# Two attentions, twice over: more of the second attention's exponentials on VectorE, by masks, under new order rules

## The chip, the cores and the metric

The kernel runs on one core of a Trainium2 chip. The metric is the device time of one execution in microseconds (us). A core has engines that run side by side, each with its own queue worked in order: TensorE (PE in the profile; PEld is its weight load), VectorE (DVE), ScalarE (ACT), GpSimd (POOL), and SyncE (SP), which here issues the DMA transfers. TensorE writes its results to PSUM, eight banks of 128 x 512 fp32; VectorE and ScalarE read them there and write to SBUF.

## The reference

x is 2048 rows of 1024 features. Four blocks follow each other; each adds its result to x. Blocks 1 and 3 are a linear attention with learned feature maps ("A"), blocks 2 and 4 a softmax attention ("B"); both use 32 heads of 32 features, and the same weights in both rounds.

```python
def _A_ref(x, wqkv, w_phi, wo):
    ...
    pq = jnp.einsum("bhsd,hdf->bhsf", q, w_phi)
    pk = jnp.einsum("bhsd,hdf->bhsf", k, w_phi)
    phi_q = jnp.concatenate([_softmax(pq, axis=-1), _softmax(-pq, axis=-1)], axis=-1)
    phi_k = jnp.concatenate([_softmax(pk, axis=-1), _softmax(-pk, axis=-1)], axis=-1)
    kv = jnp.einsum("bhsf,bhsd->bhfd", phi_k, v)
    ...
def _B_ref(x, wqkv, wo):
    ...
    scores = jnp.einsum("bhqd,bhkd->bhqk", q, k) * (Dh ** -0.5)
    p = _softmax(scores, axis=-1)
    o = jnp.einsum("bhqk,bhkd->bhqd", p, v)
    return (lambda x, *d: x.transpose(*d))(o, 0, 2, 1, 3).reshape(B, S, D) @ wo
x = x + _A_ref(_layernorm(x, axis=-1), A_wqkv, A_w_phi, A_wo)
x = x + _B_ref(_layernorm(x, axis=-1), B_wqkv, B_wo)
x = x + _A_ref(_layernorm(x, axis=-1), A_wqkv, A_w_phi, A_wo)
x = x + _B_ref(_layernorm(x, axis=-1), B_wqkv, B_wo)
```

## The kernel before

**A planner sets the order.** The body records operations (`op`: engine, planned duration, dependencies, buffers, a priority `prio`) and `Sched.run` (L145) plays them against a model of the engines: whenever an engine is free it takes the ready operation of the lowest `prio` whose buffers can be had, unless its priority lies more than WINDOW beyond the earliest work not yet begun. The order in which operations were picked is the order in which the instructions are then written, so every engine's queue is fixed beforehand. The planned durations (`act_us`, `dve_us`, `MM`) serve this order alone. Priorities count in planned microseconds of the stage: a softmax attention starts at `at`, and each of its turns is 10 units. QUOTA limits how many buffers of a class live at once. Operations marked `first` (the score groups, from the third on) go ahead of all others on TensorE. Where the plan has TensorE less than KEEP busy over SPELL, it puts in matmuls that add zero to an open accumulator (`idle_acc`, L1290).

**Two rounds of two stages.** A round ("layer") is a linear attention and then a softmax attention. The reference's 2048 rows are worked in four chunks of 512 (`qc` for queries). The keys and key states of the next round's linear attention for three chunks (`layernorm` and `a_keys` with `alone`) run inside the first softmax attention, as do its output projections.

**The softmax attention.** The 32 heads are eight groups `g` of four. A turn is one chunk of queries and one group: (qc, g). Before, the turns go over all groups with chunks 0 and 1, then chunk 2 over all groups, then chunk 3 (`turns`, L1137). A turn has two half-turns `pp`, each with eight steps d of four score tiles j: 64 tiles of 128 keys x 512 queries. A score tile is one matmul with 32 rows (row-tiled; four of them fit the array side by side). Tiles are taken in threes: three matmuls (L1034) into three banks (0 to 2 or 3 to 5 in turn), then one exponential on ScalarE of 128 x 1536 (L1042). The accumulation (L1072) multiplies the exponentials with the values and with ones, four column-tiled matmuls a step, into bank 6; at the end of a half-turn VectorE copies it to SBUF (L1087), the sums of the exponentials go through DRAM (rd) to be inverted and spread, and L1128 divides.

**Everything else passes bank 7.** Projections for later groups (`b_k`, `b_v`, `b_q`), output projections (`b_o`, in the last round `b_last`) and the next round's keys are column-tiled matmuls (L438) into bank 7 (`FIL`), read by VectorE (L867 and others). `q_away` (L884) computes the queries of chunks 2 and 3 early and stores them in DRAM (qd), `q_back` fetches them. Weights come as slabs (`slab`; class "w2" for 128 columns of a projection).

**VectorE's exponentials.** `EXTRA` names, for each turn of each round, pairs (pp, d): the two tiles j = 3 of steps d and d + 1 are taken off ScalarE's list and made by `exp_dve` (L959): a single score matmul into bank 7 (L972) for each, two operations of VectorE that read the bank (L977, L980), then six over both tiles (L983, L986, three times L991, L994). They round the scaled score to a multiple, evaluate a polynomial of the rest, and multiply by a power of two made with integer arithmetic.

Of the kernel before, what the change touches and what calls it, by code (L numbers as in the profile page):

```python
# [11 lines left out]
ALU = mybir.AluOpType  # L12
# [22 lines left out]
class Op:  # L35
    __slots__ = ("eng", "dur", "lat", "fn", "bufs", "prio", "mode", "ndep", "out", "t", "start", "seq", "accum", "first")

    def __init__(self, eng, dur, lat, fn, bufs, prio, mode, seq):
        self.eng, self.dur, self.lat, self.fn, self.bufs = eng, dur, lat, fn, bufs
        self.prio, self.mode, self.seq = prio, mode, seq  # L40
        self.ndep, self.out, self.t, self.start, self.accum, self.first = 0, [], 0.0, None, None, False
# [6 lines left out]
class Sched:  # L48
# [11 lines left out]
    def op(self, eng, dur, fn, deps=(), bufs=(), prio=0.0, lat=None, mode=None):  # L60
# [5 lines left out]
        for b in o.bufs:  # L66
            b.left += 1
        self.ops.append(o)
# [76 lines left out]
    def run(self):  # L145
# [21 lines left out]
        for o in self.ops:  # L167
            if o.ndep == 0:
                heapq.heappush(ready[o.eng], (not o.first, o.prio, o.seq, o))
        t, left, order = 0.0, len(self.ops), []  # L170
        while left:
            moved = False
            for e in engines:
# [29 lines left out]
                if pick is None:  # L203
                    continue
                if e == "PE":
# [28 lines left out]
            while events and events[0][0] <= t + 1e-9:  # L234
# [6 lines left out]
                for x in o.out:  # L241
# [4 lines left out]
                    if x.ndep == 0:  # L246
                        heapq.heappush(ready[x.eng], (not x.first, x.prio, x.seq, x))
# [10 lines left out]
LNN = 4  # L258
GATE = (1, 1)
KVG = 0.12  # L260
QUOTA = {"pk": 3, "pv": 2, "kv": 1, "ln": 2, "mm": 2, "cmp": 2, "bc": 4, "num": NUMS, "wt": 4, "fil": 2,
         "e": 6, "vp": 6, "e1": 4, "vp1": 4, "E": 6, "q2": 3, "kt": 3, "w2": 8, "w2o": 3, "oT": 26, "T": 4, "den": 2,
         "lnt": 6, "lnw": 2, "lnw1": 1, "eq": 8, "ns": 4, "cw": 6, "hl": 6, "oc": 2, "slab": 7, "slabk": 3, "fin": 4,
         "rs": 8, "pkf": 1, "cden": 2, "part": 8, "w2r": 1,
         "xs": 1, "xu": 2, "xg": 2, "xx": 2, "E1": 3}
# [3 lines left out]
ROUND = 1.5 * 2**21  # L269
POW2_D = 0.32318750170670074  # L270
POW2_0 = 0.998010015430466
POW2_C = (-2.753493604392706, 3.611980637904819, -2.738565741928622)
# [17 lines left out]
def kernel(  # L290
# [20 lines left out]
    q_scale = float(DH**-0.5 / (4 * math.log(2)))  # L311
# [379 lines left out]
    def mmg2(pb, pv, lhs, rhs, d1, d2, bufs, prio, lo=0, hi=4, more=False):  # L691
# [267 lines left out]
    def exp_dve(qc, g, pp, d, prio, kT, q_of):  # L959


        u_b, u_v = sb("xu", 2, C512, dt=F32)
        g_b, g_v = sb("xg", 2, C512, dt=F32)
        x_b, x_v = sb("xx", 2, C512, dt=F32)
        e_b, e_v = sb("E1", 2, C512)
        r = slice(96, 128)
        gs = []
        for k in range(2):
            s_b, s_v = ps("xs", FIL)

            def sfn(k=k, s_v=s_v):
                nc.tensor.matmul(  # L972
                    out=s_v(), lhsT=kT[g][1]()[r, pp, (d + k) * P:(d + k + 1) * P],
                    rhs=q_of[(qc, g)][1]()[r, (pp + 1) % 2, :], start=True, stop=True, tile_position=(96, 0))
            so = op("PE", MM, sfn, flat([kT[g][2][(d + k) // 2], q_of[(qc, g)][2]]),
                    [s_b, kT[g][0], q_of[(qc, g)][0]], prio, mode="r")
            uo = op("DVE", dve_us(512), lambda k=k, s_v=s_v: nc.vector.tensor_scalar(  # L977
                out=u_v()[:, k, :], in0=s_v(), scalar1=POW2_D, scalar2=ROUND, op0=ALU.add, op1=ALU.add),
                [so], [s_b, u_b], prio + 0.01)
            gs.append(op("DVE", dve_us(512), lambda k=k, s_v=s_v: nc.vector.scalar_tensor_tensor(  # L980
                out=g_v()[:, k, :], in0=u_v()[:, k, :], scalar=ROUND, in1=s_v(), op0=ALU.subtract, op1=ALU.subtract),
                [uo], [s_b, u_b, g_b], prio + 0.01))
        wo = op("DVE", 1024 / 1920 + 0.15, lambda: nc.vector.tensor_scalar(  # L983
            out=u_v(), in0=u_v(), scalar1=ROUND - 31.5, scalar2=ROUND + 32.0, op0=ALU.max, op1=ALU.min),
            gs, [u_b], prio + 0.02)
# [340 lines left out]
```

## Time and profile before

| | us |
|---|---|
| median of 3 runs (lowest to highest) | 2449.53 (2446.66 to 2449.86) |
| profiled execution, its own time | 2446.52 |
| its span, first to last instruction | 2444.7 |
| busy in it: TensorE / VectorE / ScalarE | 2298.8 / 1337.6 / 2128.3 |
| L1042, ScalarE's exponentials, 1332 of them | 1798.7 |
| first and last start of L1042 in the first softmax attention | 354.3 and 1308.5 |
| first and last start of L1042 overall | 354.3 and 2430.7 |

A row of a group reads: line, engine, operation, output and input tile, shapes, how often; then busy time in us and mean of one in ns; then the idle time of the engine just before them and what ended it. A row of a stretch gives its bounds and length, then the busy time of each engine with the number of instructions in brackets, the granted TensorE clock, the DMA share and GB/s. TensorE's busy time includes matmuls that overlap each other and the added zeros, so it isn't a measure of need.

### The profile page before, as it was taken

The numbers are of one execution on the slowest core, as the hardware profiler recorded it, in microseconds if no ns is written. First come the engines' busy times: TensorE is split into PE (matmuls) and PEld (weight loads), VectorE is DVE, ScalarE is ACT, GpSimd is POOL, SyncE is SP. The second block draws the span as 40 slices with busy tenths as digits, with TensorE's granted clock in tenths as the row PEclk, the third lists the DMA queues.
The fourth block names the chain that finished last, engine by engine and source line by source line (L and its number), as shares of the span: only waits on it lengthen the run. The fifth ranks groups of instructions, "written<-read, shape, count | busy, mean of one in ns | idle before, by whom it ended". The sixth has DMA issues, their size and how long they took to land.

```text
span 2444.7 us, 65791 instructions
## 1 busy us (share of the span) xinstructions
PE 2298.8 (94%) x29160; PEld 848.7 (35%) x29160; DVE 1337.6 (55%) x1775; ACT 2128.3 (87%) x1891; POOL 22.0 (1%) x70
## 2 busy tenths in 40 slices
PE   7999999999989999899999999999999998998998
PEld 4443333333333333333333333333333333333333
DVE  6986752222256635533425766322255478788863
ACT  6336569999999999999996555799999999999998
POOL 0000000000000000000000000000000000000000
PEclk9999999999999999999999999999999999999999
DMA  9210101112111122222324001111121100100000
GB/s 208 62 36 3 31 20 39 39 42 51 37 58 45 45 65 76 75 71 72 123 59 125 1 5 40 32 43 37 40 64 28 37 30 26 35 31 28 27 23 32
DMA packets 204773, 118.59 MB, mean 49 GB/s; under 512 B 122824, under 2 KB 194504, under 8 KB 203720
## 3 DMA queue, kind: packets, MB, share of 16 engines
q1 hardware_dynamic: 203432, 112.29, 17.0%
q8 instruction: 228, 3.74, 0.6%
q10 hardware_dynamic: 1056, 2.10, 0.3%
q14 instruction: 57, 0.47, 0.1%
HBM read 78.71 MB, written 16.24 MB: 39 GB/s over the span
## 4 chain that ended last, share of the span: by engine, by line
ACT 43%; PE 35%; issue 10%; DVE 7%; DMA 3%; SPq 2%; ACTq 0%; DVEq 0%
ACT arena L1042 42%; PE psum L434 19%; PE psum L1072 5%; PE psum L438 4%; PE psum L1034 4%; DVE arena L991 2%; DMA arena<-rd 1%; SPq L469 1%; PE psum L1290 1%; DVE arena L1128 1%; ACT arena L638 1%; PE psum L804 1%; PE psum L671 1%; DVE arena L977 1%; DVE arena L1087 1%
## 5 line engine op out<-in xcount | busy, mean ns | idle before, releaser
L1042 ACT ACTIVATE arena<-psum 128x1536 bf16<-128x1536 f32 x1332 | 1798.7, 1677 | 15.1 <-PE psum L1034 7.6
L1072 PE MATMUL psum<-arena 128*32 128x512 bf16 x4096 | 657.1, 385 | 8.8 <-DVE arena L1087 4.9
L1072 PE MATMUL psum<-arena,ones_bf 128*32 128x512 bf16 x4096 | 656.8, 386 | 2.3 <-issue 2.3
L1034 PE MATMUL psum<-arena 32*128 32x512 bf16 x3996 | 525.1, 383 | 97.1 <-ACT arena L1042 88.9
L438 PE MATMUL psum<-arena 128*32 128x512 bf16 x8256 | 578.6, 381 | 3.8 <-DVE arena L530 0.8
L434 PE MATMUL psum<-arena 128*128 128x512 bf16 x2032 | 472.5, 384 | 10.5 <-DVE arena L1108 3.1
L1034 PEld LDWEIGHTS <-arena 32*128 32x128 bf16 x3996 | 175.5, 91 | 624.6 <-issue 613.1
L434 PEld LDWEIGHTS <-arena 128*128 128x128 bf16 x2032 | 191.0, 98 | 268.7 <-issue 58.2
L438 PEld LDWEIGHTS <-arena 128*32 128x32 bf16 x8256 | 204.1, 96 | 211.4 <-issue 64.8
L1072 PEld LDWEIGHTS <-arena 128*32 128x32 bf16 x4096 | 156.4, 94 | 277.7 <-issue 250.8
L867 DVE CAST arena<-psum 128x512 bf16<-128x512 f32 x112 | 77.2, 689 | 259.2 <-PE psum L438 246.2
L991 DVE SCALAR_TENSOR_TENSOR arena<-arena 128x1024 f32<-128x1024 f32 x150 | 183.4, 1222 | 7.4 <-PE psum L438 2.5
L1290 PE MATMUL psum<-xT,zero 128*32 128x512 bf16 x2296 | 182.9, 380 | 0.0
L1072 PEld LDWEIGHTS <-ones_bf 128*32 128x32 bf16 x4096 | 153.9, 94 | 16.1 <-issue 7.4
L1087 DVE COPY arena<-psum 128x512 f32<-128x512 f32 x126 | 86.6, 687 | 97.3 <-PE psum L1072 96.2
L1128 DVE TENSOR_TENSOR arena<-arena 64x512 bf16<-64x512 f32 x124 | 84.6, 682 | 59.5 <-DMA arena<-rd 46.7
L638 ACT ACTIVATE arena<-psum 128x512 bf16<-128x512 f32 x80 | 42.8, 598 | 79.4 <-PE psum L434 65.7
L651 DVE TENSOR_TENSOR arena<-psum,arena 128x1024 bf16<-128x1024 f32 x64 | 78.3, 1224 | 59.2 <-PE psum L438 53.2
L977 DVE TENSOR_SCALAR arena<-psum 128x512 f32<-128x512 f32 x100 | 68.9, 689 | 69.9 <-PE psum L972 61.8
L642 DVE TENSOR_REDUCE arena<-arena 128x32 f32<-128x1024 bf16 x64 | 77.7, 1214 | 48.6 <-ACT arena L638 48.6
L761 ACT ACTIVATE arena<-psum 128x512 bf16<-128x512 f32 x128 | 69.4, 595 | 34.1 <-PE psum L434 33.6
L526 DVE TENSOR_TENSOR arena<-xT,arena 128x1024 f32<-128x1024 bf16 x64 | 77.9, 1218 | 31.3 <-ACT arena L515 31.2
(102 smaller groups left out, 1295.9 us busy)
## 6 DMA issues: line engine op xcount, KB each, us to landing
arena<-rd SPq DMA_DIRECT2D x62, 256.0 KB
arena<-in_A_wqkv_dram SPq DMA_DIRECT2D x10, 1024.0 KB
arena<-in_B_wqkv_dram SPq DMA_DIRECT2D x32, 256.0 KB
arena<-arena SPq DMA_DIRECT2D x256, 32.0 KB
arena<-in_B_wo_dram SPq DMA_DIRECT2D x32, 256.0 KB
arena<-wd_k SPq DMA_DIRECT2D x8, 1024.0 KB
arena<-in_B_wqkv_dram SPq DMA_DIRECT2D x4, 1024.0 KB
arena<-arena SPq DMA_DIRECT2D x64, 64.0 KB
```

The costliest lines, as they stand in the source:

```text
L434: nc.tensor.matmul(out_, lhsT=lhsT, rhs=rhs, start=start, stop=stop, skip_group_check=True)
L438: nc.tensor.matmul(out_[ks, :], lhsT=lhsT[:, ks], rhs=rhs, start=start, stop=stop, tile_position=(0, 32 * k), skip_group_check=True)
L526: s1 = op("DVE", dve_us(1024), lambda pr=pr, w_v=w_v: nc.vector.tensor_tensor(out=w_v(), in0=xT[:, pr, csl(c)], in1=m_v().unsqueeze(1).to_ ...
L651: ml = op("DVE", dve_us(1024), lambda vpv=vpv, wv_=wv_, sv=sv: nc.vector.tensor_tensor(out=wv_()[:, :, :, 0:DH], in0=vpv().rearrange("p (h ...
L977: uo = op("DVE", dve_us(512), lambda k=k, s_v=s_v: nc.vector.tensor_scalar(out=u_v()[:, k, :], in0=s_v(), scalar1=POW2_D, scalar2=ROUND, o ...
L991: last = [op("DVE", dve_us(1024), lambda i=i, c=c: nc.vector.scalar_tensor_tensor(out=x_v(), in0=(x_v() if i else g_v()), scalar=c, in1=g_ ...
L1034: nc.tensor.matmul(out=s_v()[:, x * C512:(x + 1) * C512], lhsT=kT[g][1]()[r, pp, d * P:(d + 1) * P], rhs=q_of[(qc, g)][1]()[r, (pp + j // ...
L1042: ex = op("ACT", act_us(w * C512), lambda s_v=s_v, e_v=e_v, w=w: nc.scalar.activation(out=e_v()[:, 0:w * C512], in_=s_v(), func=ACT.Exp, s ...
L1072: nc.tensor.matmul(out=a_v()[col:col + 32, :], lhsT=v_v()[:, kc % 4, o:o + DH] if what == 0 else ones_bf[:], rhs=ev()[:, x * C512:(x + 1) ...
L1087: cp = op("DVE", dve_us(512), lambda t_v=t_v, a_v=a_v: nc.vector.tensor_copy(out=t_v(), in_=a_v()), [last], [a_b, t_b], prio - 4)
L1128: s = [op("DVE", dve_us(512), lambda a=a, k=k, o_v=o_v, r_v=r_v, T=T: nc.vector.tensor_tensor(out=o_v()[a, :], in0=T[k][1]()[a, :], in1=r_ ...
L1290: nc.tensor.matmul(psum[32 * k:32 * k + 32, 6 * C512:7 * C512], lhsT=zero[:], rhs=xT[:, 0, 0:C512], start=False, stop=False, tile_position ...
```

## The change

- `exp_dve`: the score plus a constant is written straight as an integer whose bits are the fp32 number with the right exponent and a linear mantissa (one operation per tile reads the bank, in place of two). One operation masks the mantissa and sets the exponent of 1, one masks the exponent; a polynomial of three steps and a last multiplication follow. The scale of scores changes with it (`q_scale`, and `scale` of ScalarE's exponential).
- The pair is the two tiles j = 2, 3 of one step d, in place of j = 3 of two steps. Their accumulation steps go to the end of their half-turn.
- `EXTRA`: first softmax attention 10 pairs before, 37 after; second 40 before, 54 after.
- Order rules: VectorE's operations that read banks 6 and 7 count as 20 units earlier (`EVAC`); the later steps of a begun projection into bank 7 count as 20 earlier (`BOOST`); the single scores (`along`) may only be taken while TensorE is in row-tiled mode, or when overdue, and then rank with the score groups.
- Turns: `SIDE` chunks go side by side over the groups, 2 in the first softmax attention (as before), 3 in the second. In the second the queries of the last chunk are computed late and are no longer put away in DRAM; weights for it, and for those put away in the first, are loaded once more.
- Times of projections (`QA`, `VGAP`, `LATE`, `BO`, `OP0`, `OGAP`), quotas and the planned duration `KVG` differ.

```diff
@@ Sched.op
+        if eng == "DVE" and any(b.kind == "ps" and b.banks in ([(7,)], [(6,)]) for b in o.bufs):
+            o.ahead = EVAC
@@ Sched.run
-                heapq.heappush(ready[o.eng], (not o.first, o.prio, o.seq, o))
+                heapq.heappush(ready[o.eng], (not (o.first or o.along), o.prio - o.ahead, o.seq, o))
...
-                    if item[1] <= todo[front] + WINDOW and self._alloc(item[3].bufs):
+                    if item[3].along and mode[e] != item[3].mode and item[3].prio > now - DUE:
+                        skipped.append(item)
+                        continue
+                    if item[3].prio <= todo[front] + WINDOW and self._alloc(item[3].bufs):
...
+                if pick.first:
+                    now = pick.prio
@@
-KVG = 0.12
+DUE = 0.0
+BOOST = 20.0
+EVAC = 20.0
+QA = (40.0, 7.0)
+KVG = 0.14
...
-         ... "w2": 8, ... "oT": 26, ... "xu": 2, "xg": 2, "xx": 2, "E1": 3}
+         ... "w2": 6, ... "oT": 27, ... "xu": 2, "xg": 1, "xx": 1, "E1": 3}
...
-EXTRA = (lambda i: [(0, 2), (1, 2)] if 12 <= i < 17 else [],
-         lambda i: ([(0, 2), (1, 2)] if i % 3 else [(0, 2), (0, 5), (1, 4)]) if 16 <= i < 30 else [(i % 2, 2)] if 8 <= i < 16 else [])
+SIDE = (2, 3)
+VGAP = 7.0
+LATE = 10.0
+BO = 225
+OP0 = (233, 259, 285)
+OGAP = (3.2, 3.2, 3.2)
+EXTRA = (lambda i: [(0, 2), (1, 2)] if 10 <= i < 19 else [(1, 2)] if 2 < i < 31 else [],
+         lambda i: [(0,2),(1,4)] if 3 <= i < 30 else [])
@@ mmg2
+            if cols and i > lo:
+                last.ahead = BOOST
@@ exp_dve
-        r = slice(96, 128)
+                r = slice(64 + 32 * k, 96 + 32 * k)
...
-            so = op("PE", MM, sfn, flat([kT[g][2][(d + k) // 2], q_of[(qc, g)][2]]),
+            so = op("PE", 0.05, sfn, flat([kT[g][2][d // 2], q_of[(qc, g)][2]]),
                     [s_b, kT[g][0], q_of[(qc, g)][0]], prio, mode="r")
-            uo = op("DVE", dve_us(512), ... scalar1=POW2_D, scalar2=ROUND, op0=ALU.add, op1=ALU.add),
-            gs.append(op("DVE", dve_us(512), ... scalar=ROUND, in1=s_v(), op0=ALU.subtract, op1=ALU.subtract),
-        wo = op("DVE", 1024 / 1920 + 0.15, ... op0=ALU.max, op1=ALU.min),
-        wo = op("DVE", 1024 / 1920 + 0.15, ... op0=ALU.subtract, op1=ALU.mult), [wo], [u_b], prio + 0.02)
+            so.along = True
+            ys.append(op("DVE", dve_us(512), lambda k=k, s_v=s_v: nc.vector.tensor_scalar(
+                out=y_v()[:, k, :].bitcast(I32), in0=s_v(), scalar1=POW2_B, scalar2=0.0, op0=ALU.add, op1=ALU.max),
+                [so], [s_b, y_b], prio + 0.01))
+        mo = op("DVE", 1024 / 1920 + 0.15, lambda: nc.vector.tensor_scalar(
+            out=m_v().bitcast(I32), in0=y_v().bitcast(I32), scalar1=0x7FFFFF, scalar2=0x3F800000,
+            op0=ALU.bitwise_and, op1=ALU.bitwise_or), ys, [y_b, m_b], prio + 0.02)
+        po = op("DVE", 1024 / 1920 + 0.15, lambda: nc.vector.tensor_scalar(
+            out=y_v().bitcast(I32), in0=y_v().bitcast(I32), scalar1=0x7F800000, scalar2=None,
+            op0=ALU.bitwise_and), [mo], [y_b], prio + 0.02)
@@ attention
-                    for d in range(8):
+                    own = extra(pos[(qc, g)])
+                    order = [(d, u) for d in range(8) for u in range(2) if not (u and (pp, d) in own)]
+                    order += [(d, 1) for d in range(8) if (pp, d) in own]
+                    for n, (d, u) in enumerate(order):
@@ the rounds
+        turns = [(qc, g) for g in range(G) for qc in range(wide)] + [(qc, g) for qc in range(wide, NC) for g in range(G)]
...
-                    away = q_away(g, qc, pr + 2 + 6 * (qc - 2), w, FIL)
+                elif wide == 2:
+                    pl = at + QA[0] + QA[1] * (2 * g + qc - 2)
+                    if qc == 2:
+                        wl = slab("w2", pl - 4, B_w[:, :, g * P:(g + 1) * P], P, [away])
+                    away = q_away(g, qc, pl, wl, FIL)
                     q_of[(qc, g)] = q_back(g, qc, at + 10 * pos[(qc, g)] - 12, away)
+        if wide == 3:
+            for g in range(G):
+                pl = at + 10 * pos[(NC - 1, g)] - LATE
+                after = q_of[(NC - 1, g - 2) if g > 1 else (2, G - 1)][2][0]
+                wl = slab("w2", pl - 3, B_w[:, :, g * P:(g + 1) * P], P, [after])
+                q_of[(NC - 1, g)] = b_q(g, NC - 1, pl, wl, FIL)
...
-            bo_s = [slab("slab", at + 160 + fc, ...
+            bo_s = [slab("slab", at + BO + fc, ...
...
-                gap = (6, 6, 9)[qc]
-                p0 = (163, 200, 251)[qc]
+                gap = OGAP[qc]
+                p0 = OP0[qc]
```

More of the change, by code (lines that the diff above doesn't have):

```diff
@@ L35 @@
 class Op:
-    __slots__ = ("eng", "dur", "lat", "fn", "bufs", "prio", "mode", "ndep", "out", "t", "start", "seq", "accum", "first")
+    __slots__ = ("eng", "dur", "lat", "fn", "bufs", "prio", "mode", "ndep", "out", "t", "start", "seq", "accum", "first", "ahead", "along")
     def __init__(self, eng, dur, lat, fn, bufs, prio, mode, seq):
@@ L246, in run @@
                     if x.ndep == 0:
-                        heapq.heappush(ready[x.eng], (not x.first, x.prio, x.seq, x))
+                        heapq.heappush(ready[x.eng], (not (x.first or x.along), x.prio - x.ahead, x.seq, x))
         self.end = t
@@ L309 @@
     assert D == 1024 and S % C512 == 0
[L311 removed]
+    q_scale = float(DH**-0.5 / math.log(2) * BITS)
     A_w = A_wqkv.rearrange("(po pi) f -> pi po f", pi=P)
@@ L983, in exp_dve @@
-        wo = op("DVE", 1024 / 1920 + 0.15, lambda: nc.vector.tensor_scalar(
-            out=u_v(), in0=u_v(), scalar1=ROUND - 31.5, scalar2=ROUND + 32.0, op0=ALU.max, op1=ALU.min),
-            gs, [u_b], prio + 0.02)
-        wo = op("DVE", 1024 / 1920 + 0.15, lambda: nc.vector.tensor_scalar(
-            out=u_v().bitcast(I32), in0=u_v(), scalar1=ROUND - 31.75, scalar2=float(2**25),
-            op0=ALU.subtract, op1=ALU.mult), [wo], [u_b], prio + 0.02)
-        last = gs
+            so.along = True
@@ L1042, in attention @@
             ex = op("ACT", act_us(w * C512), lambda s_v=s_v, e_v=e_v, w=w: nc.scalar.activation(
-                out=e_v()[:, 0:w * C512], in_=s_v(), func=ACT.Exp, scale=4 * math.log(2)),
+                out=e_v()[:, 0:w * C512], in_=s_v(), func=ACT.Exp, scale=math.log(2) / BITS),
                 [so], [s_b, e_b], prio - 3)
@@ L1133, in attention @@
         return oTs, so
-    turns = [(qc, g) for g in range(G) for qc in range(2)] + [(qc, g) for qc in range(2, NC) for g in range(G)]
-    pos = {t: i for i, t in enumerate(turns)}
     xnA, xnB = {}, {}
@@ L1161 @@
         base = BASE[layer]
+        wide = SIDE[layer]
+        turns = [(qc, g) for g in range(G) for qc in range(wide)] + [(qc, g) for qc in range(wide, NC) for g in range(G)]
+        pos = {t: i for i, t in enumerate(turns)}
         second = base + (100, 45)[layer]
```

74 lines of the change are left out of this document (35 added, 39 removed).

## The prediction

> **What bounds the kernel now.** I read the page's busy strips first, then stretches of the span, then the groups by line and shape, then one piece of timeline.
>
> ```profile
> DVE  6986752222256635533425766322255478788863
> ACT  6336569999999999999996555799999999999998
> ```
>
> Two plateaus of nines on ACT are the two softmax attentions; the low parts before them are the linear attentions. The plateaus, asked as stretches (length; then busy time of PE, PEld, DVE, ACT):
>
> ```profile
> 354.30:1310.70 956.40, 896.30 (x13050) 316.28 (x13047) 389.74 (x518) 941.66 (x737) 8.31 (x24) 1.00 0.23 64
> 1540.30:2432.30 892.00, 836.71 (x11549) 290.40 (x11551) 526.46 (x676) 886.04 (x664) 0.00 (x0) 1.00 0.12 34
> ```
>
> ScalarE idles only 14.7 us and 6.0 us in them, so they last as long as ScalarE's list of work. That list is L1042, exponentials of three score tiles at once:
>
> ```profile
> L1042 ACT ACTIVATE arena<-psum 128x1536 bf16<-128x1536 f32 x1332 | 1798.7, 1677 | 15.1 <-PE psum L1034 7.6 <-PE psum L1072 7.4
> L977 DVE TENSOR_SCALAR arena<-psum 128x512 f32<-128x512 f32 x100 | 68.9, 689 | 69.9 <-PE psum L972 61.8 <-ACT arena L1042 5.8 <-PE psum L1072 1.1
> L980 DVE SCALAR_TENSOR_TENSOR arena<-arena,psum 128x512 f32<-128x512 f32 x100 | 68.7, 687 | 4.2 <-PE psum L1072 0.2
> L986 DVE TENSOR_SCALAR arena<-arena 128x1024 int32<-128x1024 f32 x50 | 34.6, 693 | 1.5
> L991 DVE SCALAR_TENSOR_TENSOR arena<-arena 128x1024 f32<-128x1024 f32 x150 | 183.4, 1222 | 7.4 <-PE psum L438 2.5 <-PE psum L1072 1.3 <-PE psum L1034 0.3
> L972 PE MATMUL psum<-arena 32*128 32x512 bf16 x100 | 38.5, 385 | 3.4 <-DVE arena L867 2.8 <-DVE arena L980 0.4
> L1087 DVE COPY arena<-psum 128x512 f32<-128x512 f32 x126 | 86.6, 687 | 97.3 <-PE psum L1072 96.2 <-ACT arena L1042 0.3
> ```
>
> One exponential is listed with 1.677 us, but neighbours overlap: the stretch 1940 to 2210 us is 270.00 us of ScalarE without a gap and touches 203 of them, some 202.5 whole, so a triple adds 1.333 us. The VectorE lines are its own exponentials and the reading of accumulators (L1087). VectorE is far from full on average; where the kernel before is densest in its exponentials, the stretch reads
>
> ```profile
> 2000.00:2360.00 360.00, 327.27 (x4468) 112.42 (x4461) 305.26 (x378) 359.35 (x269) 0.00 (x0) 1.00 0.09 29
> ```
>
> VectorE 85% busy, ScalarE without a gap worth the name. TensorE is close behind ScalarE, as one period of timeline shows:
>
> ```profile
> 2100.34 0.39 PE L1034 MATMUL psum<-arena 32*128 32x512 bf16 x3
> ...
> 2101.10 0.60 PE L438 MATMUL psum<-arena 128*32 128x512 bf16 x8
> ...
> 2101.64 0.39 PE L1034 MATMUL psum<-arena 32*128 32x512 bf16 x3
> ```
>
> From scores to scores 1.30 us, in which two accumulation steps and two projection steps ran, 0.217 us each (a step is four column-tiled matmuls). So scores and their mode switch take 1.30 - 4 x 0.217 = 0.43 us, and a triple of ScalarE covers (1.333 - 0.43)/0.217 = 4.2 steps.
>
> **ScalarE's list.** The table of pairs gives VectorE 37 pairs in place of 10 in the first attention, 54 in place of 40 in the second. A pair is two of 2048 score tiles. First: (74 - 20)/3 = 18 triples fewer, x 1.333 = -24.0 us. Second: (108 - 80)/3 = 9.33, x 1.333 = -12.4 us. The built program agrees: 1332 triples become 1304 and one double. Together -36.4 us, all on the path.
>
> **VectorE's pair.** Before: 2 x 0.689 + 2 x 0.687 + 2 x 0.693 + 4 x 1.222 = 9.03 us. After: two reads of a bank (as L977, 0.689), a mask-and-set and a mask over 1024 int32, four scalar_tensor_tensor (1.222). No row shows a bitwise operation; the nearest are L986 (one source, int32 out, 0.693) and L991 (1.222). I take 0.693, since it too has one source: 7.65 us; with the other it is 8.71. VectorE then has 390 - 90 + 283 = 583 us in about 930 (63%) and 526 - 361 + 413 = 578 us in about 879 (66%), below the 85% at which ScalarE stayed full. A turn with two pairs holds 20 triples, 26.7 us, of which the pairs take 15.3. Cost: nothing, covered by idle VectorE; without that cover 91 x 7.65 - 50 x 9.03 = 245 us. The accumulations that need a pair now come last in their half-turn, so a late pair has longer to be covered.
>
> The Trainium skill, page Vector Engine (DVE) Microarchitecture Reference, section 5.2 (Measured stream behaviour on trn2), gives 1142 ns for a one-source int32 program on 128x2048 with both ports, half of that per 1024; by it the sum stays as taken. No run so far shows it for a mask.
>
> **TensorE.** 82 more single score matmuls (L972's kind), each 0 (beside the group, in other rows of the array) to 0.385 us: 0 to 32 us of TensorE's time; near 0, because in the built order 174 of 182 stand directly behind a score group, 14 of 100 before. 27 groups fewer give back 27 x 0.43 = 12 us. The filler matmuls (L1290) go from 574 steps to 547; what remains, 547 x 0.217 = 119 us, covers it.
>
> The Trainium skill, page TensorEngine Tiling (Array Packing), section Key Properties, says that a change of tiling mode drains TensorE, which speaks against more row-tiled matmuls among column-tiled ones. The trace agrees that a switch costs (part of the 0.43 us), but the built order has 2558 switches where there were 2700, so the rule charges this change nothing.
>
> Where fillers stand says little; single triples with more than 4.2 steps do. I counted each triple's steps in both built orders and let a score group be 0.7 us late (half a triple, as scores have two sets of banks). What is beyond that: first attention 14.3 us before, 23.5 after; second 13.2 and 11.5. ScalarE's real idle before was 14.7 and 6.0, so the count is an upper bound. Of the +9.2, 2.3 us are one place early in the second turn (17 steps between two score groups, then none); I take it whole. The other 6.9 lie mostly in the last third, where ScalarE also runs 48 exponentials of the next layer's keys (0.777 us each), which give TensorE time; I take 2.2. So +4.5 us, between 0 and +9.2. Second: -1, between -1.7 and 0.
>
> **The queries put away in DRAM.** At 696 us VectorE waited 6.96 us for a buffer that the store of queries (L893) still read, the score matmul L972 behind it held TensorE's queue 2.37 us, and ScalarE lost 1.23 + 1.52 + 0.95 = 3.7 us. These queries now come one per 7 planned units and half of the stores (layer two's) are gone. -2 us, between -3.7 (gone) and +3.7 (once more elsewhere).
>
> **What costs nothing.** 16 more weight loads of 256 KB, 32 more swaps of queries and 64 fewer transfers by way of DRAM, on a queue whose transfers take 17% of the 16 engines. Output projections of layer two bunched late (3.2 units apart): 8 x 0.217 + 0.4 = 2.1 us of TensorE in about 8.5. The linear stages hold the same instructions, in another order after the first key states; TensorE idles 5.4 us from 30 to 340 us, so within 3 us either way; I take 0. After the last exponential come 12.4 us of the same work as before.
>
> **Sum.** -24.0 - 12.4 + 4.5 - 1 - 2 = -34.9. The profiled execution took 2446.5 us (span 2444.7): 2411.6. The median of the runs is 3.0 us above it; I place the forecast between, at **2413 us**. Its own ends: -36.4 - 3.7 - 1.7 - 3 gives 2402; -36.4 + 9.2 + 3.7 + 3 gives 2426.
>
> **Rivals.**
> - *TensorE becomes the bound.* The count is met in full in both attentions, 23.5 + 11.5 = 35 us of ScalarE's idle time in place of 20.7, and a stall like the one at 696 us comes in two more places: 2446.5 - 36.4 + 14.3 + 7.4 = 2432. For: stretches of 2.4 projection steps per triple had next to no filler left before. Against: 119 us of filler remain. Chance 0.11; faster, by less.
> - *Slower: TensorE's queue waits for VectorE at bank 7.* Each of 182 single scores needs the bank that VectorE read last, and VectorE runs in order behind 1.222 us operations: half of one x 0.67 busy = 0.41 us, x 182 = 75 us if it passes to ScalarE: 2446.5 - 36.4 + 75 = 2485. It decides from 36.4/182 = 0.20 us per score. Against: L972 waited 3.4 us in 100, 2.4 of them the one store. Chance 0.08.
> - *Masks run at 1.222 us.* 91 x 1.06 = 96 us more of VectorE; if a third is lost to late hand-overs, 32 us: 2444. Chance 0.05; no clear change.
> - *It doesn't do what it says* (single scores not behind the groups, or triples not fewer). The built order speaks against; 2446; chance 0.01.
>
> **Chances.** The forecast 0.75. Two times within 0.2% (5 us) can't be told apart here. Faster 0.75 + 0.11 = 0.86; same 0.05; slower 0.09 (0.08 and part of the mask case). The range runs from 2402 to 2434: the forecast's own ends, and the first rival.
>
> **What would show it.** About 1305 exponentials at the same 1.333 us; stretches some 22 and 13 us shorter; masks at 0.69 us; TensorE's waits for VectorE at the single scores under 0.2 us each. ScalarE idle over 35 us in the two stretches, or masks at 1.2 us, would prove it wrong.

## The result, and the profile after

The changed kernel takes 2418.51 us, the median of 4 runs (2417.12 to 2421.95), beside 2449.70 us for the kernel before on the same chip (2446.66 to 2449.99): 31.2 us less, a ratio of 0.988 with a 95% interval of 0.986 to 0.9895. The profiled executions differ by less, 2446.52 and 2419.81 us, which is 26.7 us. The accounting below is made between those two; the 4.5 us by which the medians differ more is spread between executions.

The busy strips of the changed kernel's page, VectorE and ScalarE:

```profile
DVE  6986662444679777666646666366786587566763
ACT  6336559999999999999996555899999999999998
```

ScalarE's two plateaus of nines are as before; VectorE is fuller on both. The same two attentions, as stretches from the start of the first triple to the start of the small activation that follows the last one, L1124 (L1104 before) (length; then busy time of PE, PEld, DVE, ACT and POOL; the granted clock, 1.00; DMA share and GB/s):

```profile
354.56:1291.55 936.99, 886.95 (x12975) 312.22 (x12975) 567.89 (x714) 917.87 (x719) 12.53 (x24) 1.00 0.24 67
1521.67:2407.35 885.68, 828.56 (x11543) 286.58 (x11542) 567.36 (x709) 874.48 (x654) 0.00 (x0) 1.00 0.12 32
```

Between the same marks before has 956.43 us with 941.66 of ScalarE's work, and 892.45 with 885.99. So the first attention is 19.4 us shorter and the second 6.8; what lies before, between and behind them changed by +0.3, -0.8 and less than 0.1: together -26.7. ScalarE's own work fell by 23.8 and 11.5 us, so the new list is in the time nearly in full. But its idle time (length less work) rose, from 14.8 to 19.1 us in the first and from 6.5 to 11.2 in the second, and that took 9.1 us back.

The groups by line and shape of the changed kernel (busy us and mean ns; then the idle time just before them and what ended it):

```profile
L1059 ACT ACTIVATE arena<-psum 128x1536 bf16<-128x1536 f32 x1304 | 1762.4, 1630 | 25.2 <-PE psum L1051 12.5 <-PE psum L1092 8.5 <-DVE arena L1008 1.2
L997 DVE TENSOR_SCALAR arena<-psum 128x512 int32<-128x512 f32 x182 | 125.1, 687 | 99.6 <-PE psum L990 88.4 <-PE psum L1051 9.3 <-ACT arena L1059 1.0
L990 PE MATMUL psum<-arena 32*128 32x512 bf16 x182 | 68.5, 376 | 2.7 <-DVE xT L945 1.1 <-DVE arena L667 0.7 <-DVE arena L997 0.6
L1003 DVE TENSOR_SCALAR arena<-arena 128x1024 int32<-128x1024 int32 x91 | 62.7, 689 | 1.9
L1000 DVE TENSOR_SCALAR arena<-arena 128x1024 int32<-128x1024 int32 x91 | 62.7, 689 | 4.9 <-PE psum L1092 0.7 <-DVE arena L997 0.4 <-ACT arena L1059 0.2
L1092 PE MATMUL psum<-arena 128*32 128x512 bf16 x4096 | 626.9, 384 | 14.3 <-DVE arena L1107 11.9 <-ACT arena L1059 1.1
```

L1059 are the triples: 1304, as the forecast said. L1000 and L1003 are the two mask operations, 0.689 us each. L997 reads the bank that the single score L990 filled: VectorE waits for the score (88.4 us, idle time that costs nothing here), not the score for VectorE. All 182 scores together waited 2.7 us, 0.015 us each. L1092 waited 11.9 us for the accumulator copies of L1107 (4.9 before).

Where the added idle time sits is seen in the timeline (start, length, engine and line; in brackets how long the engine had waited, and for what). Three places of the first attention:

```profile
392.42 21.60 ACT L1059 ACTIVATE arena<-psum 128x1536 bf16<-128x1536 f32 x16 [1.97 <-PE psum L1051]
...
993.77 1.45 ACT L1059 ACTIVATE arena<-psum 128x1536 bf16<-128x1536 f32 x1 [1.40 <-PE psum L1092]
...
996.59 2.79 ACT L1059 ACTIVATE arena<-psum 128x1536 bf16<-128x1536 f32 x2 [1.36 <-PE psum L1092]
```

The first is the place early in the second turn, with 17 steps between two score groups: 1.97 us, forecast 2.3. The other two are in the last third. And one place of the second attention:

```profile
2100.34 2.00 SPq L554 DMA_DIRECT2D arena<-in_B_wo_dram  x2
2102.38 4.49 SPq L554 DMA_DIRECT2D arena<-in_B_wqkv_dram  x2
...
2103.05 0.68 DVE L1107 COPY arena<-psum 128x512 f32<-128x512 f32 x1
...
2106.98 3.12 SPq L1137 DMA_DIRECT2D arena<-arena  x2
...
2110.96 0.81 PE L454 MATMUL psum<-arena 128*32 128x512 bf16 x8 [3.44 <-DMA arena<-in_B_wqkv_dram]
2112.39 0.25 DVE L1142 RECIPROCAL arena<-arena 128x16 f32<-128x16 f32 x1 [5.72 <-DMA arena<-arena]
2112.42 1.45 ACT L1059 ACTIVATE arena<-psum 128x1536 bf16<-128x1536 f32 x1 [3.57 <-PE psum L1051]
```

The two output weights of layer two (1 MB each, first line) are issued just ahead of a late query weight and of the small transfers of the sums (L1137, 2 KB). The sums are in SBUF at 2103.73 us, when the copy L1107 ends, but SyncE is still issuing the weights (4.49 us for these two) and begins with the sums only at 2106.98. TensorE then stands 3.44 us at a projection whose weight is still on its way, VectorE 5.72 us at the reciprocal (L1142) whose sums are, and ScalarE 3.57 us at scores that come behind the projection.

### The profile page after: what moved, and what is told of

Same layout as the page of the kernel before. It is cut to its first block, busy times and chain, and to the rows that moved or that the text cites. A ratio compares the mean times of both kernels' runs of the same rounds, so it can differ in the third digit from the quotient of the medians.

```text
span 2418.0 us, 65660 instructions
## 1 busy us (share of the span) xinstructions
PE 2273.7 (94%) x28986; PEld 842.0 (35%) x29056; DVE 1557.7 (64%) x2003; ACT 2093.0 (87%) x1864; POOL 26.2 (1%) x70
## 5 line engine op out<-in xcount | busy, mean ns | idle before, releaser
L1059 ACT ACTIVATE arena<-psum 128x1536 bf16<-128x1536 f32 x1305 | 1763.3, 1629 | 25.2 <-PE psum L1051 12.5
L1092 PE MATMUL psum<-arena 128*32 128x512 bf16 x4096 | 626.9, 384 | 14.3 <-DVE arena L1107 11.9
L1092 PE MATMUL psum<-arena,ones_bf 128*32 128x512 bf16 x4096 | 627.4, 384 | 2.4 <-issue 2.4
L1051 PE MATMUL psum<-arena 32*128 32x512 bf16 x3914 | 521.2, 383 | 79.9 <-ACT arena L1059 71.4
L454 PE MATMUL psum<-arena 128*32 128x512 bf16 x8256 | 569.5, 383 | 7.6 <-DMA arena<-in_B_wqkv_dram 3.4
L450 PE MATMUL psum<-arena 128*128 128x512 bf16 x1970 | 463.1, 382 | 16.4 <-DVE arena L1128 4.0
L1051 PEld LDWEIGHTS <-arena 32*128 32x128 bf16 x3914 | 169.3, 91 | 609.9 <-issue 598.6
L1008 DVE SCALAR_TENSOR_TENSOR arena<-arena 128x1024 f32<-128x1024 f32 x273 | 332.7, 1219 | 5.6 <-PE psum L1092 0.9
L454 PEld LDWEIGHTS <-arena 128*32 128x32 bf16 x8256 | 184.9, 96 | 233.6 <-issue 109.1
L1092 PEld LDWEIGHTS <-arena 128*32 128x32 bf16 x4096 | 162.2, 95 | 268.1 <-issue 216.4
L997 DVE TENSOR_SCALAR arena<-psum 128x512 int32<-128x512 f32 x182 | 125.1, 687 | 99.6 <-PE psum L990 88.4
L1092 PEld LDWEIGHTS <-ones_bf 128*32 128x32 bf16 x4096 | 158.4, 95 | 33.5 <-issue 17.5
L1322 PE MATMUL psum<-xT,zero 128*32 128x512 bf16 x2188 | 166.3, 379 | 0.0
L1107 DVE COPY arena<-psum 128x512 f32<-128x512 f32 x126 | 86.4, 686 | 57.7 <-PE psum L1092 55.7
L1011 DVE SCALAR_TENSOR_TENSOR arena<-arena 128x1024 bf16<-128x1024 f32 x91 | 111.2, 1222 | 5.7 <-PE psum L1092 1.0
L654 ACT ACTIVATE arena<-psum 128x512 bf16<-128x512 f32 x80 | 42.8, 599 | 79.8 <-PE psum L450 66.1
```

The source lines that it names most:

```text
L450: nc.tensor.matmul(out_, lhsT=lhsT, rhs=rhs, start=start, stop=stop, skip_group_check=True)
L454: nc.tensor.matmul(out_[ks, :], lhsT=lhsT[:, ks], rhs=rhs, start=start, stop=stop, tile_position=(0, 32 * k), skip_group_check=True)
L997: ys.append(op("DVE", dve_us(512), lambda k=k, s_v=s_v: nc.vector.tensor_scalar(out=y_v()[:, k, :].bitcast(I32), in0=s_v(), scalar1=POW2_B ...
L1008: last = [op("DVE", dve_us(1024), lambda i=i, c=c: nc.vector.scalar_tensor_tensor(out=x_v(), in0=(x_v() if i else m_v()), scalar=c, in1=m_ ...
L1011: eo = op("DVE", dve_us(1024), lambda: nc.vector.scalar_tensor_tensor(out=e_v(), in0=x_v(), scalar=POW2_0, in1=y_v(), op0=ALU.add, op1=ALU ...
L1051: nc.tensor.matmul(out=s_v()[:, x * C512:(x + 1) * C512], lhsT=kT[g][1]()[r, pp, d * P:(d + 1) * P], rhs=q_of[(qc, g)][1]()[r, (pp + j // ...
```

## The experiments

Each run's two attentions are given between those marks as length/idle time of ScalarE: 956.4/14.8, 892.5/6.5 for before, 937.0/19.1, 885.7/11.2 for after. The theory: the time is ScalarE's list plus its idle time; the new order rules and VectorE's cheaper pair only make the shorter list possible.

**The old number of pairs under the new rules.** Pairs back to 10 and 40:

```diff
-EXTRA = (lambda i: [(0, 2), (1, 2)] if 10 <= i < 19 else [(1, 2)] if 2 < i < 31 else [],
-         lambda i: [(0,2),(1,4)] if 3 <= i < 30 else [])
+EXTRA = (lambda i: [(0, 2), (1, 2)] if 12 <= i < 17 else [],
+         lambda i: [(0, 2), (1, 4)] if 10 <= i < 30 else [])
```

> The changed kernel with the old numbers of pairs: 10 in the first softmax attention (turns 12 to 16, as before), 40 in the second (two in each of turns 10 to 29), in the new form and under the new rules. ScalarE gets back 18 + 9.3 triples x 1.333 us = 36.4 us. If the gain is ScalarE's shorter list (my theory): 2418.5 + 36 = 2455, about the time before (2449.7) plus what the new order costs, 2448 to 2458. If the order rules and turns bring the gain themselves: about 2420 to 2430.

Measured: 2456.95 us (7 runs, 2453.48 to 2460.26), ratio to before 1.003 (1.0019 to 1.0041); 954.6/12.6, 900.2/13.8. Its triples, by line and shape:

```profile
L1059 ACT ACTIVATE arena<-psum 128x1536 bf16<-128x1536 f32 x1332 | 1799.8, 1639 | 21.1 <-PE psum L1051 9.4 <-DVE arena L1008 5.7 <-PE psum L1092 4.0
```

1332 triples again, and 38.4 us slower than after. ScalarE's work in the stretches (length less idle) is 942.0 and 886.4 us, 24.1 and 11.9 above after: 36.0 of the 38.4. So the gain is ScalarE's shorter list. The new rules, masks and turns with the old list gain nothing: about 7 us slower than before, mostly as idle time in the second attention (5.7 us of it a wait for VectorE's L1008).

**More pairs under the old rules.** The kernel before with the second attention's 54 pairs, in the old arithmetic; and the same with the new arithmetic (masks in both attentions; the pair still j = 3 of two steps, no new rule of order or turns). The list of pairs, the same in both:

```diff
-         lambda i: ([(0, 2), (1, 2)] if i % 3 else [(0, 2), (0, 5), (1, 4)]) if 16 <= i < 30 else [(i % 2, 2)] if 8 <= i < 16 else [])
+         lambda i: [(0,2),(1,4)] if 3 <= i < 30 else [])
```

> The kernel before with the changed list of pairs in the second softmax attention only, 54 in place of 40, in the old form (9.03 us each) and under the old rules and turns. ScalarE's list is 9.33 triples x 1.333 = 12.4 us shorter. If only ScalarE's list counts: 2449.7 - 12.4 = 2437. If the old form and rules can't feed more pairs (the new rules are what makes the room): 2444 or more, with new idle time of ScalarE in the second attention.

> The kernel of e2 (old rules and turns, 54 pairs in the second attention) with the masked arithmetic, 7.65 us a pair in place of 9.03, in the old geometry. If the dearer pair made e2 slow: about 2437 to 2445. If TensorE and bank 7 did, loaded by the projections of two chunks side by side in the first turns: above 2480, ScalarE still losing 50 us or more between 1640 and 2000 us.

Measured: 2509.19 us (4 runs, 2508.63 to 2514.05), ratio 1.0247 (1.0233 to 1.0261), 959.6/17.8, 954.5/75.7 with the old arithmetic; 2478.35 us (4 runs, 2475.16 to 2479.52), ratio 1.0118 (1.0105 to 1.0132), 955.1/13.6, 924.6/45.9 with the new. Both are slower than before although their list is shorter. The second run falls between its two expectations: far above 2445, but just below 2480 and with less idle time than was set, so TensorE and bank 7 are not shown to be the cause. Two stretches of the one with the old arithmetic, early and late in the second attention (columns as above):

```profile
1640.00:2000.00 360.00, 334.09 (x4703) 124.13 (x4695) 248.73 (x315) 292.95 (x216) 0.00 (x0) 1.00 0.13 36
2040.00:2440.00 400.00, 371.11 (x5096) 128.93 (x5088) 318.04 (x395) 399.13 (x298) 0.00 (x0) 1.00 0.10 29
```

The early one with the new arithmetic:

```profile
1640.00:2000.00 360.00, 336.09 (x4668) 121.00 (x4665) 242.71 (x300) 320.36 (x236) 0.00 (x0) 1.00 0.14 38
```

The same of before:

```profile
1640.00:2000.00 360.00, 344.18 (x4728) 118.11 (x4723) 164.45 (x222) 360.00 (x269) 0.00 (x0) 1.00 0.15 41
```

And of after, 20 us earlier as its second attention starts 20 us earlier:

```profile
1620.00:1980.00 360.00, 335.81 (x4556) 112.68 (x4553) 250.26 (x313) 359.05 (x268) 0.00 (x0) 1.00 0.11 30
```

All the loss is in the early turns: ScalarE works 292.95 of 360 us there, 399.13 of 400 later. VectorE's average says little, since it is the same 69% in the one that loses 67 us as in after, which loses 1. In that stretch before holds 1824 projection matmuls (L438) and after only 1344 (L454), since the new turns spread them; in before these turns have few pairs, and ScalarE no gap. The cheaper pair is worth 30.8 us of it (2509.19 less 2478.35). The rest, 40 us of idle time, goes only with the new turns and rules. What ScalarE waits for in that stretch, with the old arithmetic (total us, number, longest), is mostly the accumulation, not the scores:

```profile
ACT arena L1042 <- PE psum L1072: 57.4, 34, 3.5
```

With the new arithmetic it is 33.7 us of 39.6. TensorE was not full there: it ran 960 and 660 matmuls that add zero, where after ran 648. Which of the changes removes the wait, the sparser projections or the rules, was not separated: no kernel with the new turns alone, or with two chunks side by side, ran. Four of the rules were taken out or weakened one at a time (below), and none of these runs has more than 3.2 us of idle time above after in the second attention, so no single one of them is seen to explain the 40 us.

**One more operation per pair.** A fifth operation of 1.22 us for each of the 91 pairs, whose result is overwritten by the next one:

```diff
+        mo = op("DVE", dve_us(1024), lambda: nc.vector.scalar_tensor_tensor(out=x_v(), in0=m_v(), scalar=1.0,
+                in1=m_v(), op0=ALU.add, op1=ALU.mult), [mo], [m_b, x_b], prio + 0.02)
         last = [mo]
```

> The changed kernel with one more scalar_tensor_tensor of 1.222 us in every pair (its result is overwritten): 91 x 1.22 = 111 us more of VectorE, 8.87 us a pair, about the old form's price. If VectorE's idle time covers it (my theory): within 5 us of 2418.5. If late hand-overs by VectorE are already what makes ScalarE idle: 2430 or more, with more of TensorE's waits for L1107's copies.

Measured: 2428.08 us (4 runs, 2425.69 to 2431.06), ratio 0.9908 (0.9893 to 0.9923); 950.6/31.2, 881.8/7.6. Of the 111 us added to VectorE (91 x 1.222), 9.6 came through: the first attention is 13.6 us longer, the second 3.9 us shorter, as it lost its stall at 2110 us when the longer pair moved the order around. This lies between the two expectations, and TensorE waited less for the accumulator copies than in after (6.7 us, 11.9 there), so the named rival isn't seen. VectorE is not the bound, and its cover is not complete either; how much of the loss is order and how much cover isn't shown.

**The rules of order, one at a time.** VectorE's scores not held behind a score group; reads of a bank 10 units ahead and not 20; begun projections 5 ahead and not 20; and accumulation in order of d, the pairs not last (with scores led by 8 units):

```diff
-            so.along = True
-            so = op("PE", 0.05, sfn, ...
+            so = op("PE", MM, sfn, ...
...
-EVAC = 20.0
+EVAC = 10.0
...
-BOOST = 20.0
+BOOST = 5.0
...
-                    order = [(d, u) for d in range(8) for u in range(2) if not (u and (pp, d) in own)]
-                    order += [(d, 1) for d in range(8) if (pp, d) in own]
+                    order = [(d, u) for d in range(8) for u in range(2)]
```

> The changed kernel without the rule that puts VectorE's single scores behind ScalarE's score groups (planned at a matmul's full length, by priority alone). More switches between row and column tiling: up to 168 more places x 2 x 0.11 us = 37 us of TensorE, for which 119 us of added zeros give cover. If TensorE's filler covers it: within 6 us of 2418.5. If this rule makes the room for the pairs: 2435 or more, ScalarE's idle time before L1059 above 40 us (25.2 now).

> The changed kernel with VectorE's reads of banks 6 and 7 only 10 units ahead in place of 20. Theory: half the lead is still more than the distance of a pair's operations (5 units), so no change, 2414 to 2424. If late reads of the banks cost ScalarE: 2430 or more with longer waits of TensorE for L1107 (11.9 us now).

> The changed kernel with the later steps of a begun projection only 5 units ahead in place of 20. If finishing begun projections is what frees bank 7 for the single scores: slower, 2425 or more. If not: within 5 us of 2418.5.

> The changed kernel with a pair's accumulation steps in the order of d, as before, and the pairs' priority 8 units ahead in place of 5. By the count of steps the excess is the same (24.6 and 6.6 us). If a late pair needs the place at the end: slower by 8 us or more, with ScalarE waiting for accumulations (L1090) that wait for VectorE. If not: within 5 us of after.

Measured, with after run twice:

```
                         us (lowest to highest, runs)      ratio to before (95%)      stretches/idle
after                    2418.51 (2417.12-2421.95, 4)      0.988  (0.986-0.9895)      937.0/19.1, 885.7/11.2
after again              2420.22 (2416.65-2425.09, 5)      0.9886 (0.9872-0.9901)     940.4/22.2, 885.5/11.2
scores not held          2432.97 (2429.84-2436.86, 6)      0.9938 (0.9926-0.995)      945.9/27.2, 888.7/14.4
bank reads 10            2424.48 (2423.56-2425.15, 4)      0.9902 (0.989-0.9915)      944.2/25.7, 880.0/5.6
begun projections 5      2439.90 (2437.49-2441.46, 5)      0.9965 (0.9953-0.9977)     959.3/38.5, 884.4/10.1
accumulation by d        2434.42 (2429.98-2438.13, 6)      0.9945 (0.9932-0.9959)     949.0/30.8, 883.7/10.1
```

In each the list is the same and the added time is ScalarE's idle time, mostly in the first attention. The scores not held miss both of their expectations: more than 6 us are lost, but the time is below 2435 us and the idle time before the triples is 34.3 us, not above 40. For them, the loads of the single score's operand (by line and shape):

```profile
L990 PEld LDWEIGHTS <-arena 32*128 32x128 bf16 x182 | 16.5, 91 | 65.1 <-issue 62.0 <-DMA arena<-arena 3.1
```

and the same of after:

```profile
L990 PEld LDWEIGHTS <-arena 32*128 32x128 bf16 x182 | 16.7, 92 | 3.7 <-issue 3.7
```

The weight load of the first score in a row-tiled stretch of TensorE's queue stands, and no releaser explains it. In this run 168 of the 182 single scores are the first of their stretch (57 alone, the others ahead of a group), in after 8. So most of the 62.0 us moved here from the groups' own loads, which stand 563.6 us in place of 598.6; the sum of both rose by 23 us, and loads standing is not yet TensorE's time.

What it costs TensorE can be measured in the gapless stretches of the traces, from the last column-tiled matmul's start to the next one's, less a step of 0.217 us (medians): 0.42 us for a group, 0.42 for a single score alone, 0.63 in after for a group with a score behind it, 0.67 in this run for a group with a score, mostly ahead of it. An estimate from these and the counts is 40 us for the 182 scores in after and 56 here. The Trainium skill, page TensorEngine Tiling (Array Packing), section Key Properties, says that a change of tiling mode drains TensorE; that a score alone costs as much as a group agrees with it. The filler matmuls, which were to cover this, fell from 2188 to 1904, 15 us at 0.217 us for four, as the planner counts these scores and switches too. The kernel is 14 us slower; how TensorE's 16 us become idle time of ScalarE although fillers gave way is not shown.

With begun projections at 5, the waits of ScalarE in the first attention (what waited, for what; total us, number, longest) include:

```profile
ACT arena L1059 <- PE psum L1092: 12.4, 14, 1.9
ACT arena L654 <- DVE arena L651: 7.5, 4, 3.5
```

In after the first of these is 7.5 us, and the second isn't there. The second is the next layer's keys: ScalarE's activation L654 stands for VectorE, and the triples behind it stand too. The single scores waited 3.3 us in all (2.7 in after), so that they lack bank 7, as the expectation had it, isn't shown. For accumulation by d, the triples:

```profile
L1059 ACT ACTIVATE arena<-psum 128x1536 bf16<-128x1536 f32 x1304 | 1761.5, 1636 | 35.8 <-PE psum L1051 20.3 <-PE psum L1091 9.3 <-PE psum L454 5.8
```

It loses 14 to 16 us, but waits for scores (L1051) more than for accumulation (L1091); with the lead changed as well, it is no clean proof of the rule. Bank reads at 10 cost 4 to 7 us in the first attention, by the two profiles of after, and happened to lose the stall at 2110 us: no verdict.

**The stall at 2110 us.** First the two output weights 3 units later, behind the query weight:

```diff
-BO = 225
+BO = 228
```

> The changed kernel with the two 1 MB loads of the output weights of the last round due 3 units later, behind the first late load of query weights, in place of just ahead of it. The trace of after has TensorE waiting 3.4 us for that query load at 2111 us and ScalarE idle 4.8 us in that slice. If the queue of loads makes this stall: it goes, 2418.5 - 4.5 = 2414, ScalarE's idle time in the second attention 12.2 - 4.8 = 7.4 us. If the late projection itself is too late: no change, 2417 to 2420.

Measured: 2421.98 us (4 runs, 2416.99 to 2424.13), ratio 0.9883 (0.987 to 0.9897); 940.3/22.1, 885.9/11.4. Nothing gained. Its timeline there:

```profile
2103.11 2.02 SPq L554 DMA_DIRECT2D arena<-in_B_wo_dram  x2
2107.76 4.01 SPq L1137 DMA_DIRECT2D arena<-arena  x2
...
2115.47 0.25 DVE L1142 RECIPROCAL arena<-arena 128x16 f32<-128x16 f32 x1 [6.00 <-DMA arena<-arena]
...
2118.20 4.13 ACT L1059 ACTIVATE arena<-psum 128x1536 bf16<-128x1536 f32 x3 [4.66 <-issue]
```

TensorE's weight is in time now, but the sums of L1137 are still behind the two bulk loads: VectorE waits 6.00 us for them, the pair behind them ends at 2118.12 us, and ScalarE, idle for 4.66 us, starts its triple at 2118.20. The stall has two legs, and one was left. So the same loads were cut into eight of 256 KB, 1.5 units apart:

```diff
-            bo_s = [slab("slab", at + BO + fc, B_o[:, :, fc * C512:(fc + 1) * C512], C512, [q_of[(2, G - 1)][2][0]])
-                    for fc in range(2)]
+            bo_s = []
+            for fc in range(2):
+                b_, v_ = sb("slab", PO, C512)
+                bo_s.append((b_, v_, [dma(at + 225 + 1.5 * (4 * fc + i), lambda fc=fc, i=i, v_=v_: nc.sync.dma_start(
+                    out=v_()[:, 2 * i:2 * i + 2, :], in_=B_o[:, 2 * i:2 * i + 2, fc * C512:(fc + 1) * C512]),
+                    [q_of[(2, G - 1)][2][0]], [b_], kb=256) for i in range(4)]))
```

> The changed kernel with the two 1 MB loads of the last output weights cut into eight of 256 KB, issued 1.5 units (4 us) apart. The trace of e3 shows that the stall near 2110 us stays when only the query weights go first: VectorE's reciprocal of the sums then waited 6.0 us for its 2 KB transfer, and the pair behind it was late. If the bulk ahead of small transfers makes the stall: ScalarE's idle time in the second attention falls from 12.2 to about 6 us, 2418.5 - 6 = 2412. If the late projection does: no change.

> The changed kernel as it is, beside the next three on the same chip: 2415 to 2422, for a fair comparison.

Measured: 2415.31 us (4 runs, 2413.17 to 2421.5), ratio 0.9869 (0.9855 to 0.9884); 936.0/17.9, 879.7/5.7. The changed kernel as it is, again: 2420.22, in the table above. The place in the split one:

```profile
2099.07 2.04 SPq L1270 DMA_DIRECT2D arena<-in_B_wo_dram  x2
2101.16 0.47 SPq L554 DMA_DIRECT2D arena<-in_B_wqkv_dram  x1
2101.68 1.60 SPq L1270 DMA_DIRECT2D arena<-in_B_wo_dram  x3
2103.38 1.18 SPq L1137 DMA_DIRECT2D arena<-arena  x2
...
2107.82 0.25 DVE L1142 RECIPROCAL arena<-arena 128x16 f32<-128x16 f32 x1 [1.29 <-DMA arena<-arena]
```

The pieces were issued back to back in twos and threes, not 4 us apart: five ahead of the sums, three behind them. So how much comes from smaller loads and how much from less of them ahead was not separated. The reciprocal waits 1.29 us in place of 5.72, and ScalarE's work between 2080 and 2130 us rises from

```profile
2080.00:2130.00 50.00, 42.53 (x554) 13.98 (x552) 28.05 (x34) 45.20 (x35) 0.00 (x0) 0.97 0.24 68
```

in after to

```profile
2080.00:2130.00 50.00, 44.98 (x601) 15.12 (x598) 30.41 (x38) 49.61 (x38) 0.00 (x0) 1.00 0.27 76
```

The second attention took 885.7 and 885.5 us in the two profiles of after and takes 879.7 here: 6 us, as expected, and its idle time, 5.7 us, is near the 6.5 of before. The Trainium skill, page Perfetto Trace Analysis, section DMA Optimizations, says that transfers cut into smaller ones may let some start sooner; here it is the small transfers behind them that do. The median is the lowest of all kernels run, but its interval overlaps that of after, so by timing alone it is not a better kernel; the profiles place the 6 us, and the next run, with the same pieces, has 880.5 us there too.

**Can the rest be read from the order?** On top of the split loads, the next round's keys of chunks 1 and 2 a few units later, by the count of steps 3.7 us less of idle time:

```diff
-for c, p0 in ((0, 190), (1, 220), (2, 265)):
+for c, p0 in ((0, 190), (1, 224), (2, 270)):
```

> The kernel of e8 (output weights in eight small loads) with the next round's keys of chunks 1 and 2 due 4 and 5 units later in the first softmax attention. Counted by steps between score groups as in the prediction, the excess there falls from 23.5 to 19.8 us. If the count tells ScalarE's idle time there: 3 to 4 us faster than e8, about 2412. If not: 2415.

Measured: 2423.43 us (5 runs, 2422.03 to 2427.66), ratio 0.9902 (0.9889 to 0.9915); 949.3/29.3, 880.5/6.2. A miss: the first attention is 13.3 us longer than with the split loads alone and idles 11.4 us more. The waits of ScalarE in it include

```profile
ACT arena L1059 <- PE psum L1051: 10.7, 14, 2.0
ACT arena L654 <- DVE arena L651: 3.0, 1, 3.0
```

where the split loads alone had 5.0 us of the first and none of the second. The second is a wait of ScalarE for VectorE, and the count knows of TensorE's steps alone. It names places where scores come late; it does not rank two orders that differ by a few us.

## Why the prediction was right, and where it was off

The forecast was 2413 us, 36.5 below the median before; the median after is 2418.51, within the range and the forecast's own ends. Part of that is luck: between the profiled executions the terms missed by 8.2 us (2411.6 forecast, 2419.8 measured), and the median is nearer mostly because the medians happen to lie further apart. The two attentions are 19.4 and 6.8 us shorter, where some 22 and 13 were forecast. Term by term, in us between the two profiled executions (rounded terms, hence 26.8 for 26.7):

```
                               forecast   measured
ScalarE's list, first           -24.0      -23.8
ScalarE's list, second          -12.4      -11.5
its idle time, first        +4.5 - 2        +4.3
its idle time, second            -1         +4.7
linear stages and the end         0         -0.5
sum                             -34.9      -26.8
```

- *The list* was right in count (1304 triples and one double) and in price: the gapless 240.00 us from 420 to 660 us touch 180 triples, some 179.5 whole, 1.337 each where 1.333 was used. The old counts put 36 us back, so this is shown.
- *VectorE's pair* was sized right: masks at 0.689 us where 0.693 was taken; VectorE's work 568 and 567 us in the attentions, where 583 and 578 were forecast. "Covered by idle VectorE" is nearly right: the run with 111 us more of it lost 9.6 us, so the cover in the first attention may be thinner than an average of 61% busy suggests; that run moved the order too.
- *TensorE.* The single scores added near the low end of their bounds, but not for the reason given. A score behind a group isn't free: it adds 0.21 us (0.63 less 0.42). Before, with 33 of its 100 scores alone at 0.42 us and the rest mostly ahead of a group (0.71 us with it), they cost an estimated 34 us; the 182 now cost 40, 6 us more, which doesn't show in the time. Without the rule that holds them behind a group the kernel was 14 us slower.
- *The count of steps in the first attention.* 392 us and the last third were named rightly. The gain of 2 us at the queries' stores didn't come: the stretch from 694 to 752 us still lost 1.04 + 1.30 + 1.09 + 0.29 + 0.36 = 4.1 us, where before lost 3.7 at 696. As a net the two terms (+2.5) came near the +4.3, but two executions of the same program differ by 3 us here (19.1 and 22.2), so the agreement is partly luck and no proof of the count, and the run that trusted it most missed by more than 10 us.
- *The step that failed* is in "What costs nothing": the 16 more weight loads, on a queue of which only the mean load (17%) was looked at. The change also moves the two 1 MB output weights from 160 to 225 units, and there they stand ahead of a query weight and of 2 KB sums that are needed at once. Forecast 0, and -1 for the second attention's idle time, which rose by 4.7. The stall is 6 us, by the run without it; there the idle time is 5.7 us, 0.8 less than before, so the -1 fits but for the stall. The later loads showed the second leg, the split ones that the stall goes when five pieces and not both loads are issued ahead of the sums.
- *The rivals.* TensorE's wait at bank 7 needed 0.20 us per score and had 0.015. Masks at 1.222 us: 0.689. Not doing what it says: 1304 triples. TensorE as the bound: its queue does end most of ScalarE's waits, but the two attentions idle 30.3 us (33.4 in the second profile of after), under the 35 that the prediction set, and the largest single stall was a transfer's.

What stays open: why the new turns and rules give the early turns of the second attention room for pairs (the old ones lose 40 us even with the cheap pair, waiting for accumulations), and how much of the first attention's 19 us of idle time is a property of the order and how much of one execution.

## What to carry to other kernels

When one engine has no gap, count its list and price an entry by a gapless stretch and not by its listed duration; that part of a forecast holds to a microsecond. Then follow every transfer that the change issues at another time, look at what is queued right behind it, and try bulk loads that stand ahead of small urgent ones in pieces. A planned order that is made anew moved stalls of 4 to 20 us elsewhere in these runs, whatever the edit was for: such differences are measured, not counted.

## What the runs showed of the hardware

- With two loads of 1 MB (and query weights) ahead on one queue, VectorE waited 5.72 and 6.00 us for 2 KB transfers; with the same bytes in pieces of 256 KB, five ahead and three behind, 1.29 us. The issue of the two small transfers itself took 3.12 and 4.01 us behind the bulk, and 1.18 behind the pieces. The Trainium skill, page DMA: Bandwidth & Descriptors, section Queues, rings and completion order, says that each of the DMA engines takes the descriptors of one ring in order; this agrees, though no run here looked at the single engines.
- Masks over 128 x 1024 int32 in SBUF took as long as arithmetic with one source: 0.689 us for both forms (0.693 before for a clamp and for a subtraction with a multiplication).
- A single row-tiled score among column-tiled matmuls took TensorE 0.42 us, as much as a group of three; behind such a group it added 0.21 us, and 0.30 in before, where most stood ahead of the group.
